# RWKV-5 attention and a routed expert layer on one core: attention output by chunk parity and head, states carried on TensorE and ScalarE

## The chip, the core and the metric

The kernel runs on one core of one Trainium2 chip. The metric is the device time of one execution in microseconds (us). Three executions of the kernel before took 550.02, 550.48 and 550.54 us, so its time is the median, 550.48 us. The profile is of one more execution, which took 550.23 us.

The engines are called as in the profile: PE is TensorE, PEld its weight loads, DVE is VectorE, ACT is ScalarE, POOL is GpSimd, SP issues transfers. An f32 matmul of the program leaves two records in the profile (it runs as two passes), a PE transpose leaves one.

## What is computed

The first part is RWKV-5 attention with 4 batches, 8 heads, 768 tokens and a head width of 48:

```python
for t in range(S):
    kt, vt, rt = (k[:, :, t], v[:, :, t], r[:, :, t])
    cur = np.einsum('bhd,bhe->bhde', u[None] * kt, vt)
    y[:, :, t] = np.einsum('bhd,bhde->bhe', rt, state + cur)
    state = w[None, :, :, None] * state + np.einsum('bhd,bhe->bhde', kt, vt)
```

The second part takes y as x (4 x 768 tokens, 384 wide). It forms nine logits for each token (eight experts and one local gate), picks an expert by the largest logit or keeps the token before's expert where the gate says so, sends each token through its expert (384 to 1024, relu, 1024 to 384) and scales the result by the softmax probability.

## The kernel before

There are three stages: attention (`chunked_attention`), routing (`route`) and the experts (`experts`). Only the attention stage is changed, with the layout of its inputs. All work is in f32.

Attention runs over 16 **items**, each one batch and one pair of heads. The two heads of a pair lie on partitions 0 to 47 and 64 to 111; each head is padded from 48 to 64 (`DP`). The 768 tokens are cut into six chunks of 128. Powers of the decay w are made once at the start (`pw`, its reciprocal `inv`, and `endT`, which weights a key by what is left of it at the end of its chunk).

For one item `first` does this:

- POOL scales r by `pw` into `rw` (L112), k by `endT` into `ke` (L114), and multiplies r and k into `pd` (L115). DVE scales k by `inv` into `kw` (L113).
- PE forms what each of five chunks adds to the state, for both heads at once, into `ds` (L120). DVE then walks the recurrence: for each chunk and head it multiplies the state by w to the 128th and adds `ds` (L128 for the first chunk, L130 for the four others), into `st`. The state tile is block-diagonal, 128 x 128 with zeros between the heads.
- PE forms the scores inside each chunk, one head on each half of the array's rows (`sc`, L141), and DVE masks them into `am` (L144).
- PE sums `pd` weighted by u (`dp`, L152), and DVE multiplies that by v transposed into `own` (L154): the token's own term.

`second` follows one item later. PE applies the states to `rw` (`yp`, L163) and the masked scores to v, one head on each half of the array's columns (`yp`, L169). DVE adds `own` and writes `xT` (L172). After the four items of a batch `finish` turns `xT` by 24 PE transposes (`tp`, L180), ACT copies them into `x` (L181), which goes to memory, eight matmuls form the nine logits (`lp`, L189), ACT copies them (`lT`, L191), six small transposes turn them (`lq`, L194), and DVE writes `lt` (L196).

Each item's five inputs (rT, kT, k, v, vT, all padded to 64 per head, 384 KB each) are loaded by SP into one of three buffers. Eight PSUM banks are shared by all the matmul outputs of the stage. A scheduler decides the final order of the instructions on each engine from the order in which the program writes them.

## Time and profile before

| what | number |
|---|---|
| median of three executions | 550.48 us |
| the profiled execution | 550.23 us |
| its span, first to last instruction | 548.5 us |
| busy share of the span: PE, DVE, POOL, ACT | 89%, 36%, 29%, 10% |
| first `ds` matmul of the first item | 19.19 us |
| `lt` of the last batch written (end of attention) | 182.20 + 0.21 us |
| mean granted TensorE clock | 0.952 |

The span has 1.7 us around it. Attention takes the first 182 us, routing with the first gathers lasts until 221.8 us, and the experts fill the rest with PE busy throughout. The clock is granted in full through the attention stage, at half during most of routing.

A timeline row gives the start, the time from the start of a run of like instructions to the end of its last one, the engine, the line, and how many records it merges. Matmuls are pipelined, so such rows overlap: what a group costs on PE is the distance from its start to the start of the next group.

### The profile page before, as it was taken

The numbers are of one execution on the slowest core, as the hardware profiler recorded it, in microseconds if no ns is written. First come the engines' busy times: TensorE is split into PE (matmuls) and PEld (weight loads), VectorE is DVE, ScalarE is ACT, GpSimd is POOL, SyncE is SP. The second block draws the span as 40 slices with busy tenths as digits, with TensorE's granted clock in tenths as the row PEclk, the third lists the DMA queues.
The fourth block names the chain that finished last, engine by engine and source line by source line (L and its number), as shares of the span: only waits on it lengthen the run. The fifth ranks groups of instructions, "written<-read, shape, count | busy, mean of one in ns | idle before, by whom it ended". The sixth has DMA issues, their size and how long they took to land.

```text
span 548.5 us, 6145 instructions
## 1 busy us (share of the span) xinstructions
PE 487.6 (89%) x2358; PEld 291.7 (53%) x2358; DVE 197.4 (36%) x467; ACT 55.7 (10%) x106; POOL 161.1 (29%) x138
## 2 busy tenths in 40 slices
PE   0689999999999435999999999999999999999990
PEld 0577677577577134455555555555555555555540
DVE  6799859769765561001111111112011111111010
ACT  0000200200201000011111101111101111011110
POOL 6678547357320113302122121221221210201102
PEclk9999999999999755799999999999999999999995
DMA  8678866755410841203514306206117016000001
GB/s 293 244 260 269 270 212 240 241 192 192 141 33 23 346 178 50 79 9 104 197 34 157 137 27 208 92 25 246 56 30 272 28 36 232 29 1 23 14 2 52
DMA packets 21653, 72.34 MB, mean 132 GB/s; under 512 B 3543, under 2 KB 6778, under 8 KB 19568
## 3 DMA queue, kind: packets, MB, share of 16 engines
q1 hardware_dynamic: 13824, 56.63, 29.4%
q0 software_dynamic: 3840, 10.23, 5.7%
q10 hardware_dynamic: 3952, 5.00, 2.5%
q8 instruction: 21, 0.34, 0.3%
q14 instruction: 16, 0.13, 0.1%
HBM read 62.41 MB, written 10.22 MB: 132 GB/s over the span
## 4 chain that ended last, share of the span: by engine, by line
issue 52%; DVE 18%; PE 15%; POOL 12%; DMA 1%; POOLq 1%; ACT 0%
POOL out_dram L544 6%; DVE st L130 5%; POOL xg L500 5%; PE lp L189 4%; DVE kw L113 4%; DVE am L144 4%; PE mp L461 2%; PE tp L180 2%; PE yp L169 2%; DVE xT L172 2%; DVE own L154 2%; PE yp L163 2%; PE ds L120 1%; PE sc L141 1%; DVE st L128 1%
## 5 line engine op out<-in xcount | busy, mean ns | idle before, releaser
L518 PE MATMUL h<-exT,w1t 128*128 128x448 f32 x384 | 155.6, 545 | 0.0
L528 PE MATMUL y<-hT,w2t 128*128 128x448 f32 x384 | 155.4, 541 | 0.0
L518 PEld LDWEIGHTS h<-exT,w1t 128*128 128x128 f32 x384 | 72.2, 193 | 64.7 <-issue 64.7
L528 PEld LDWEIGHTS y<-hT,w2t 128*128 128x128 f32 x384 | 70.2, 190 | 58.8 <-issue 58.3
L544 POOL DMA_INDIRECT out_dram<-yo,sid x32 | 31.3, 978 | 174.6 <-DVE yo L542 174.0
L513 DVE COPY exT<-etp 128x384 f32<-128x384 f32 (+1 forms) x32 | 16.2, 508 | 132.6 <-PE etp L512 131.7
L521 ACT ACTIVATE hT<-h 128x448 f32<-128x448 f32 x64 | 34.8, 544 | 285.4 <-PE h L518 242.9
L542 DVE TENSOR_SCALAR yo<-otp,gate 128x384 f32<-128x384 f32 (+1 forms) x32 | 19.5, 615 | 118.7 <-PE otp L540 118.6
L500 POOL DMA_INDIRECT xg<-x_d,gid x32 | 32.4, 1013 | 101.4 <-PE etp L512 85.4
L112 POOL TENSOR_TENSOR rw<-rT,pw 128x768 f32<-128x768 f32 x16 | 28.8, 1798 | 43.2 <-PE yp L163 42.3
L130 DVE SCALAR_TENSOR_TENSOR st<-st,pw,ds 64x64 f32<-64x64 f32 x128 | 35.9, 280 | 4.1
L115 POOL TENSOR_TENSOR pd<-rT,kT 128x768 f32<-128x768 f32 x16 | 29.8, 1860 | 16.5 <-PE dp L152 12.5
L114 POOL TENSOR_TENSOR ke<-k,endT 128x768 f32<-128x768 f32 x16 | 32.5, 2031 | 6.7 <-POOL rw L112 3.1
L144 DVE TENSOR_TENSOR am<-sc,mask 128x384 f32<-128x384 f32 x64 | 31.2, 551 | 0.5
L141 PE MATMUL sc<-rw,kw 64*128 64x128 f32 x384 | 27.1, 290 | 2.3 <-POOL rw L112 2.3
L169 PE MATMUL yp<-am,v 128*64 128x128 f32 x384 | 28.9, 281 | 0.0
L120 PE MATMUL ds<-v,ke 128*128 128x128 f32 x160 | 23.1, 294 | 6.0 <-POOL ke L114 6.0
L163 PE MATMUL yp<-rw,st 128*128 128x128 f32 x160 | 25.5, 290 | 1.4 <-DVE st L130 1.4
L141 PEld LDWEIGHTS sc<-rw,kw 64*128 64x128 f32 x384 | 23.9, 196 | 4.4 <-POOL rw L112 2.6
L163 PEld LDWEIGHTS yp<-rw,st 128*128 128x128 f32 x160 | 20.8, 190 | 9.0 <-PE dp L152 4.2
L181 ACT COPY x<-tp 128x384 f32<-128x384 f32 x24 | 11.2, 480 | 141.8 <-PE tp L180 141.6
L152 PE MATMUL dp<-pd,uz 128*128 128x384 f32 x64 | 25.0, 513 | 0.0
(132 smaller groups left out, 308.6 us busy)
## 6 DMA issues: line engine op xcount, KB each, us to landing
w1t<-in_w_dram SPq DMA_DIRECT2D x8, 1536.0 KB, 6.6
w2t<-in_w_dram SPq DMA_DIRECT2D x8, 1536.0 KB, 8.4
rT<-in_rT_dram SPq DMA_DIRECT2D x16, 384.0 KB, 4.8
kT<-in_kT_dram SPq DMA_DIRECT2D x16, 384.0 KB, 5.8
k<-in_k_dram SPq DMA_DIRECT2D x16, 384.0 KB, 6.2
v<-in_v_dram SPq DMA_DIRECT2D x16, 384.0 KB, 4.1
vT<-in_vT_dram SPq DMA_DIRECT2D x16, 384.0 KB, 3.3
x_d<-x ACTq DMA_DIRECT2D x4, 1152.0 KB, 6.0
```

What stands on the lines that cost most here:

```text
L114: nc.gpsimd.tensor_mul(ke, t["k"], spread(endT[:, hp], 1, NCH))
L115: nc.gpsimd.tensor_mul(pd, t["rT"], t["kT"])
L130: nc.vector.scalar_tensor_tensor(state[q, c, i], state[q, c - 1, i], pw[q, hp, P:P + 1], add, Alu.mult, Alu.add)
L141: nc.tensor.matmul(sc[i][:, c * P:(c + 1) * P], lhsT=kw[q, g + c, :], rhs=rw[q, g + c, :], start=True, stop=True)
L144: nc.vector.tensor_mul(am[:, i, g:g + 3], sc[i][:, :3 * P].rearrange("p (c t) -> p c t", t=P), spread(mask, 1, 3))
L163: nc.tensor.matmul(yp[:, c % 3 * P:(c % 3 + 1) * P], lhsT=t["state"][:, c - 1].rearrange("p i e -> p (i e)"), rhs=t["rw"][:, c, :], start= ...
L169: nc.tensor.matmul(yp[i * DP:(i + 1) * DP, c % 3 * P:(c % 3 + 1) * P], lhsT=t["v"][:, c, i * DP:(i + 1) * DP], rhs=t["am"][:, i, c, :], st ...
L500: nc.gpsimd.indirect_dma_start(out=xg[:n], out_offset=None, in_=x_d, in_offset=bass.IndirectOffsetOnAxis(ap=gid[:n, e * ST + j:e * ST + j ...
L518: nc.tensor.matmul(h[:, :CAP], lhsT=t[e]["w1"][:, m, kk, :], rhs=t[e]["xT"][:, kk, :], start=(kk == 0), stop=(kk == DK - 1))
L521: nc.scalar.activation(hT, h[:, :CAP], Act.Relu)
L528: nc.tensor.matmul(t[e]["y"][d][:, :CAP], lhsT=t[e]["w2"][:, m, d * P:(d + 1) * P], rhs=t[e][m], start=(m == 0), stop=(m == FK - 1))
L544: nc.gpsimd.indirect_dma_start(out=outs[c], out_offset=bass.IndirectOffsetOnAxis(ap=sid[:n, c:c + 1], axis=0), in_=yo[:n], in_offset=None, ...
```

## The change

Attention is written anew around quarters of the array.

- **Tokens by chunk parity.** The output y of one head takes one PSUM bank: even chunks on partitions 0 to 63, odd chunks on 64 to 127. So `inside` (scores times v) uses one half of the array's columns for each parity, and `before` (states times `rw`) and `own` (u times `pd`) use quarters: 64 rows (a head) by 64 columns (a parity). `xT` holds 8 heads by 384 columns in place of 4 pairs by 768.
- **States on PE and ACT.** The state has 64 rows by 64 columns for each head, with no zero blocks. `added` forms the five additions into one bank `T` (64 x 64 for each matmul) and ACT copies the first one out to `S`. `chain(n, c)` multiplies `S` of the chunk before by a diagonal of w to the 128th (`wd`) on PE, accumulating onto `T`, and ACT copies the sum to `S`. DVE no longer touches the states.
- **Logits** of a batch are 16 matmuls with 32 columns each, two row halves by four column groups; `gather` adds the parts by multiplying with `sel`.
- **Turning** is done by `turn` for each item (six transposes, two ACT copies) and not for a whole batch.
- **Loads.** r and k come in one tile and transfer (`rk`), k and v by token without padding (`kv`), and v transposed by parity (`vT`), in four buffers. From the fifth item on, `rk` and `vT` are loaded as two transfers of 48 partitions each, which leaves the padding rows of the first loads in place. `ke` has 576 columns in place of 768.
- The program order of an iteration n is set in the loop at the end: `turn(n-2)`, `added(n)`, `inside(n-1)`, `chain 1`, `before(n-1)`, `chain 2`, `own(n)`, `chain 3`, half of the scores, `chain 4`, the other half; then `logits` or `gather` in the iterations that follow a batch.
- The input layout, made on the host, and the fallback for unusual decays read the new tensors; the fallback does not run on these inputs.

```diff
-        ps = pool("ps", 8, space=PSUM)
+        three = pool("three", 3)
+        ps = pool("ps", 7, space=PSUM)
+        pst = pool("pst", 1, space=PSUM)
...
+        def load(n):
+            b, hp = divmod(n, HP)
+            rk, vT, kv = rks[n % NB], vTs[n % NB], kvs[n % NB]
+            for t, src in ((rk, rk_d), (vT, vT_d)):
+                flat = t.rearrange("p a c t -> p (a c t)")
+                if n < NB:
+                    nc.sync.dma_start(out=flat, in_=src[b, hp])
+                else:
+                    for i in range(2):
+                        q = slice(i * DP, i * DP + DH)
+                        nc.sync.dma_start(out=flat[q], in_=src[b, hp, q])
+                if t is rk:
+                    nc.sync.dma_start(out=kv, in_=kv_d[b, hp])
...
-        sts = [once.tile([P, NCH - 1, 2, DP], F32, name=f"st{i}") for i in range(2)]
-        for z in sts:
-            for i in range(2):
-                nc.gpsimd.memset(z[i * DP:(i + 1) * DP, :, 1 - i, :], 0.0)
...
+        endT = once.tile([P, HP, 2, DH], F32, name="endT")
...
+        halves = once.tile([P, DP], F32, name="halves")
+        nc.vector.tensor_add(halves, ident[:, :DP], ident[:, DP:])
+        wd = once.tile([P, HP, DP], F32, name="wd")
+        nc.vector.tensor_mul(wd, spread(halves, 1, HP), pw[:, :, P:P + 1].to_broadcast([P, HP, DP]))
+        sel = once.tile([P, E + 1], F32, name="sel")
+        nc.vector.tensor_reduce(sel, ident.rearrange("p (j i) -> p i j", j=4)[:, :E + 1], axis=AX.X, op=Alu.add)
...
+        def scale(n):
+            t = items[n]
+            t["ke"] = two.tile([P, NCH, 2 * DH], F32, name="ke")
+            t["pd"] = two.tile([P, NCH, P], F32, name="pd")
+            t["rw"] = three.tile([P, NCH, P], F32, name="rw")
+            hp = t["hp"]
+            nc.gpsimd.tensor_mul(t["ke"], t["k"], spread(endT[:, hp].rearrange("p i d -> p (i d)"), 1, NCH))
+            nc.gpsimd.tensor_mul(t["pd"], t["rT"], t["kT"])
+            nc.gpsimd.tensor_mul(t["rw"], t["rT"], spread(pw[:, hp, :P], 1, NCH))
+        def added(n):
+            t = items[n]
+            t["kw"] = two.tile([P, NCH, P], F32, name="kw")
+            nc.vector.tensor_mul(t["kw"], t["kT"], spread(inv[:, t["hp"]], 1, NCH))
+            t["T"] = pst.tile([P, NCH - 1, DP], F32, name="T")
+            t["S"] = three.tile([P, NCH - 1, DP], F32, name="S")
             for c in range(NCH - 1):
+                for h in range(2):
+                    nc.tensor.matmul(t["T"][h * DP:(h + 1) * DP, c], lhsT=t["ke"][:].rearrange("p c x -> p (c x)")
+                                     [:, (2 * c + h) * DH:(2 * c + h) * DH + DP],
+                                     rhs=t["v"][:, (2 * c + h) * DH:(2 * c + h) * DH + DP],
+                                     start=(c == 0), stop=(c == 0), skip_group_check=True)
+            nc.scalar.copy(t["S"][:, 0], t["T"][:, 0])
...
+        def chain(n, c):
+            t = items[n]
+            for h in range(2):
+                q = slice(h * DP, h * DP + DH)
+                nc.tensor.matmul(t["T"][h * DP:(h + 1) * DP, c], lhsT=wd[q, t["hp"]], rhs=t["S"][q, c - 1],
+                                 start=False, stop=True, skip_group_check=True)
+            nc.scalar.copy(t["S"][:, c], t["T"][:, c])
...
+        def own(n):
+            for p in range(2):
+                for h in range(2):
+                    q = slice(h * DP, h * DP + DH)
+                    nc.tensor.matmul(dp[h][p * DP:(p + 1) * DP, :C2 * P].rearrange("p (c t) -> p c t", c=C2),
+                                     lhsT=w_t[q, t["hp"], 1:2].to_broadcast([DH, DP]),
+                                     rhs=t["pd"][q].rearrange("p (c k) t -> p k c t", k=2)[:, p],
+                                     start=True, stop=True)
...
+        def scores(n, g):
+            sc = [bank("sc") for _ in range(2)]
+            for c in range(3):
+                for h in range(2):
+                    q = slice(h * DP, h * DP + DH)
+                    nc.tensor.matmul(sc[h][:, c * P:(c + 1) * P], lhsT=t["kw"][q, 3 * g + c],
+                                     rhs=t["rw"][q, 3 * g + c], start=True, stop=True)
...
+        def inside(n):
+            t = items[n]
+            t["y"] = [bank("yp") for _ in range(2)]
+            for h in range(2):
+                for c in range(NCH):
+                    p, c2 = c % 2, c // 2
+                    nc.tensor.matmul(t["y"][h][p * DP:(p + 1) * DP, c2 * P:(c2 + 1) * P],
+                                     lhsT=t["v"][:, (2 * c + h) * DH:(2 * c + h) * DH + DP], rhs=t["am"][:, h, c],
+                                     start=(c2 == 0), stop=False, skip_group_check=True)
...
+        def before(n, xT):
+            t = items[n]
+            for c in range(1, NCH):
+                p, c2 = c % 2, c // 2
+                for h in range(2):
+                    q = slice(h * DP, h * DP + DH)
+                    nc.tensor.matmul(t["y"][h][p * DP:(p + 1) * DP, c2 * P:(c2 + 1) * P],
+                                     lhsT=t["S"][q, c - 1], rhs=t["rw"][q, c],
+                                     start=False, stop=True, skip_group_check=True)
+            for h in range(2):
+                nc.vector.tensor_add(xT[:, 2 * t["hp"] + h], t["y"][h][:, :C2 * P],
+                                     t["own"][:, h].rearrange("p c t -> p (c t)"))
...
+        def turn(n, xT, x):
+            for h in range(2 * items[n]["hp"], 2 * items[n]["hp"] + 2):
                 tp = bank("tp")
-                for hp in range(HP):
-                    nc.tensor.transpose(tp[:, hp * P:(hp + 1) * P], xT[:, hp, c * P:(c + 1) * P], ident)
-                nc.scalar.copy(x[:, c].rearrange("p (h e) -> p h e", h=H),
-                               tp.rearrange("p (h e) -> p h e", h=H)[:, :, :DH])
+                for c2 in range(C2):
+                    nc.tensor.transpose(tp[:, c2 * P:(c2 + 1) * P], xT[:, h, c2 * P:(c2 + 1) * P], ident)
+                nc.scalar.copy(x[:, :, h * DH:(h + 1) * DH],
+                               tp[:, :C2 * P].rearrange("p (c e) -> p c e", e=DP)[..., :DH])
...
-            lT = two.tile([E + 1, S], F32, name="lT")
-            for g in range(2):
-                z = slice(g * S // 2, (g + 1) * S // 2)
-                lp = bank("lp")
-                for hp in range(HP):
-                    nc.tensor.matmul(lp[:E + 1, :S // 2], lhsT=wp[:, hp, :], rhs=xT[:, hp, z],
-                                     start=(hp == 0), stop=(hp == HP - 1))
+            lT = two.tile([P, 2, C2 * P], F32, name="lT")
+            lp = [bank("lp") for _ in range(2)]
+            for h in range(H):
+                for p in range(2):
+                    q, j = slice(p * DP, (p + 1) * DP), h % 4
+                    nc.tensor.matmul(lp[p][32 * j:32 * j + 32, :C2 * P], lhsT=wp[q, h], rhs=xT[q, h],
+                                     start=(h < 4), stop=(h >= 4))
+            for p in range(2):
+                nc.scalar.copy(lT[:, p], lp[p][:, :C2 * P])
...
+        def gather(b, lT):
             lq = bank("lq")
             for c in range(NCH):
-                nc.tensor.transpose(lq[:, c * (E + 1):(c + 1) * (E + 1)], lT[:, c * P:(c + 1) * P],
-                                    ident[:E + 1, :E + 1])
-            nc.vector.tensor_copy(lt[:, b * NCH:(b + 1) * NCH, :].rearrange("p c e -> p (c e)"),
-                                  lq[:, :NCH * (E + 1)])
+                nc.tensor.matmul(lq[:, c * (E + 1):(c + 1) * (E + 1)], lhsT=lT[:, c % 2, c // 2 * P:(c // 2 + 1) * P],
+                                 rhs=sel, start=True, stop=True)
+            nc.scalar.copy(lt[:, b * NCH:(b + 1) * NCH, :].rearrange("p c e -> p (c e)"), lq[:, :NCH * (E + 1)])
...
+        scale(0)
+        for n in range(M + 2):
+            if n + 2 < M:
+                load(n + 2)
+            if n - 2 >= 0:
+                b = items[n - 2]["b"]
+                turn(n - 2, xTs[b], xs[b])
+            if n < M:
+                added(n)
+                if n % HP == 0:
+                    xTs[n // HP] = two.tile([P, H, C2 * P], F32, name="xT")
+                    xs[n // HP] = two.tile([P, NCH, D], F32, name="x")
+            if n + 1 < M:
+                scale(n + 1)
+            if 0 <= n - 1 < M:
+                inside(n - 1)
+            if n < M:
+                chain(n, 1)
+            if 0 <= n - 1 < M:
+                before(n - 1, xTs[items[n - 1]["b"]])
+            if n < M:
+                chain(n, 2)
+                own(n)
+                chain(n, 3)
+                scores(n, 0)
+                chain(n, 4)
+                scores(n, 1)
+            if n >= 2 and (n - 2) % HP == HP - 1:
+                b = items[n - 2]["b"]
+                lTs[b] = logits(b, xTs[b], xs[b])
+                if n == M + 1:
+                    gather(b, lTs[b])
+            elif n - 3 >= 0 and (n - 3) % HP == HP - 1:
+                gather(items[n - 3]["b"], lTs[items[n - 3]["b"]])
```

In the order of PE's instructions, an item between two batch ends stood like this before (`st_108` and `st_109` are the two state tiles):

```order
L120 MATMUL ds<-v,ke 128x128 x5
L141 MATMUL sc<-rw,kw 128x128 x12
L152 MATMUL dp<-pd,uz 128x384 x2
L163 MATMUL yp<-rw,st_108 128x128 x2
L169 MATMUL yp<-am,v 64x128 x6
L163 MATMUL yp<-rw,st_108 128x128 x3
L169 MATMUL yp<-am,v 64x128 x6
```

and stands like this now (`T` from `kv` and `ke` is `added`, `T` from `S` and `wd` is a `chain` step, `yp` from `kv` is `inside`, `yp` from `S` is `before`, `dp` is `own`):

```order
L222 MATMUL tp<-ident,xT 128x128 x6
L148 MATMUL T<-kv_117,ke 64x64 x10
L200 MATMUL yp<-am,kv_116 64x128 x12
L159 MATMUL T<-S,wd 64x64 x2
L210 MATMUL yp<-rw,S 64x128 x10
L159 MATMUL T<-S,wd 64x64 x2
L171 MATMUL dp<-pd,w_t 64x384 x4
L159 MATMUL T<-S,wd 64x64 x2
L188 MATMUL sc<-rw,kw 128x128 x6
L159 MATMUL T<-S,wd 64x64 x2
L188 MATMUL sc<-rw,kw 128x128 x6
```

The transposes of the item two back come first; the four chain steps stand apart, each with other matmuls of PE behind it; the output shape (the first number is the rows written) changes six times in an item, as often as before.

In the iteration that also forms a batch's logits, PE's order is this now, behind the transposes, `added` and `inside`:

```order
L210 MATMUL yp<-rw,S 64x128 x10
L171 MATMUL dp<-pd,w_t 64x384 x2
L159 MATMUL T<-S,wd 64x64 x2
L171 MATMUL dp<-pd,w_t 64x384 x2
L188 MATMUL sc<-rw,kw 128x128 x2
L159 MATMUL T<-S,wd 64x64 x2
L188 MATMUL sc<-rw,kw 128x128 x2
L159 MATMUL T<-S,wd 64x64 x2
L188 MATMUL sc<-rw,kw 128x128 x2
L159 MATMUL T<-S,wd 64x64 x2
L188 MATMUL sc<-rw,kw 128x128 x6
L233 MATMUL lp<-xT,wp 32x384 x16
```

Here the scheduler has put the chain later: three of its steps stand inside the scores, two score matmuls apart.

At the start of the stage DVE's order before was

```order
L89 RECIPROCAL inv<-pw 128x512
L91 TENSOR_TENSOR end<-inv,pw 128x512
L113 TENSOR_TENSOR kw<-kT,inv 128x768 x2
L96 COPY endT<-ep 128x512
L128 COPY st_108<-ds 64x64 x2
```

and it is now (`halves`, `wd` and `sel` are the new constants)

```order
L112 RECIPROCAL inv<-pw 128x512
L122 TENSOR_TENSOR halves<-ident 128x64
L114 TENSOR_TENSOR end<-inv,pw 128x512
L124 TENSOR_TENSOR wd<-halves,pw 128x256
L126 TENSOR_REDUCE sel<-ident 128x9
L143 TENSOR_TENSOR kw<-rk_107,inv 128x768
L119 COPY endT<-ep 128x384
L143 TENSOR_TENSOR kw<-rk_108,inv 128x768
```

`endT`, for which the first `ke` on POOL waits, has moved ahead of the second `kw`.

178 lines of the change are left out of this document (54 added, 124 removed).

## The prediction

> **What bounds the kernel now.** I began with the table of busy time by stretch, because the change touches only the first 182 us.
>
> ```profile
> core 0: us, PE busy (x) PEld busy (x) DVE busy (x) ACT busy (x) POOL busy (x), PEclk, DMA share, GB/s
> 40.00:60.00 20.00, 19.46 (x206) 15.89 (x202) 19.36 (x45) 0.00 (x0) 16.56 (x9) 1.00 0.82 277
> 60.00:80.00 20.00, 19.28 (x145) 12.28 (x142) 11.93 (x35) 3.77 (x8) 7.39 (x5) 1.00 0.73 240
> ```
>
> Two kinds of stretch alternate. Between batch ends PE and DVE are both nearly full (19.46 and 19.36 of 20 us); at a batch end PE stays full while DVE falls to 11.93 us and POOL to 7.39. So DVE can at most be the second bound, and a batch end costs PE time that nothing else shares. The timeline prices each group. The last two items and the end of attention, with the start behind them:
>
> ```profile
> 155.53 1.38 PE L120 MATMUL ds<-v,ke 128*128 128x128 f32 x10
> ...
> 162.78 1.38 PE L120 MATMUL ds<-v,ke 128*128 128x128 f32 x10
> 163.76 0.48 DVE L128 COPY st<-ds 64x64 f32<-64x64 f32 x2 [0.30 <-PE ds L120]
> 164.10 1.61 PE L141 MATMUL sc<-rw,kw 64*128 64x128 f32 x24
> 164.26 2.47 DVE L130 SCALAR_TENSOR_TENSOR st<-st,pw,ds 64x64 f32<-64x64 f32 x8
> 165.63 1.56 PE L152 MATMUL dp<-pd,uz 128*128 128x384 f32 x4
> 166.76 1.95 DVE L144 TENSOR_TENSOR am<-sc,mask 128x384 f32<-128x384 f32 x4
> 167.03 0.61 PE L163 MATMUL yp<-rw,st 128*128 128x128 f32 x4
> 167.57 0.88 PE L169 MATMUL yp<-am,v 128*64 128x128 f32 x12
> 168.37 0.94 PE L163 MATMUL yp<-rw,st 128*128 128x128 f32 x6
> 168.63 1.01 DVE L154 TENSOR_TENSOR own<-dp,vT 128x384 f32<-128x384 f32 x2
> 169.24 0.88 PE L169 MATMUL yp<-am,v 128*64 128x128 f32 x12
> 169.56 1.16 DVE L172 TENSOR_TENSOR xT<-yp,own 128x384 f32<-128x384 f32 x2
> ...
> 173.16 2.84 PE L180 MATMUL tp<-ident,xT 128*128 128x128 f32 x24
> 175.93 5.33 PE L189 MATMUL lp<-xT,wp 128*9 128x384 f32 x16
> 181.19 0.35 PE L194 MATMUL lq<-ident,lT 9*128 9x9 f32 x3
> 181.30 0.47 ACT L191 COPY lT<-lp 9x384 f32<-9x384 f32 x1 [2.11 <-PE lp L189]
> 181.82 0.35 PE L194 MATMUL lq<-ident,lT 9*128 9x9 f32 x3 [0.28 <-ACT lT L191]
> 182.20 0.21 DVE L196 COPY lt<-lq 128x54 f32<-128x54 f32 x1 [8.37 <-PE lq L194]
> ```
>
> ```profile
> 11.88 4.77 DVE L113 TENSOR_TENSOR kw<-kT,inv 128x768 f32<-128x768 f32 x2
> 16.58 0.68 DVE L96 COPY endT<-ep 128x512 f32<-128x512 f32 x1
> 17.33 3.57 POOL L114 TENSOR_TENSOR ke<-k,endT 128x768 f32<-128x768 f32 x2 [1.49 <-DVE endT L96]
> 19.19 2.50 PE L120 MATMUL ds<-v,ke 128*128 128x128 f32 x10 [6.00 <-POOL ke L114]
> ...
> 25.97 1.28 PE L120 MATMUL ds<-v,ke 128*128 128x128 f32 x10
> ```
>
> Read starts, not lengths. A plain item takes 162.78 - 155.53 = 7.25 us, with PE's groups close behind each other. From the second item's `ds` (25.97) to the last one's (162.78) are 136.8 us for 14 items, 9.77 each: the batch ends hold the difference. Such an end is 24 transposes (173.16 to 175.93, 2.77 us), 16 logit passes (to 181.19, 5.26 us), and about 1.2 us to `lt`. Attention ends at 182.41, 19.6 us after the last `ds`.
>
> **Prices.** A full-array pass of 128 columns costs 2.77 / 24 = 0.115 us, one of 384 columns 5.26 / 16 = 0.33. The 24 score passes, on the two row halves by turns, take 164.10 to 165.63 = 1.53 us; one at a time they would be 2.76, two at once 1.38. So halves run at the same time, and about 0.15 us is left for the change of shape. The column halves agree (12 passes, 167.57 to 168.37, 0.80 us: 0.69 + 0.11), and so does `ds` (10 passes, 1.32: 1.15 + 0.17). I take 0.15 for each change of shape. A pass of 64 columns isn't in the trace: half of 0.115 is 0.06, and three `lq` records of 9 columns take 0.35, so at most 0.12; I take 0.08, nearer to the wide pass by size.
>
> **The new item on PE**, in its order, from these prices:
>
> - `turn`: 6 transposes, 0.69 + 0.15 = 0.84 (moved out of the batch end, not added).
> - `added`: 20 short passes in column pairs, 10 x 0.08 + 0.15 = 0.95 (0.75 to 1.35).
> - `inside`: 24 passes in pairs, same shape, 12 x 0.115 = 1.38.
> - Four `chain` steps of two passes in time, 0.16 each; the first and the last change the shape: 0.94.
> - `before`: 20 passes over four quarters, at most six on one: 0.69. In pairs it would be 1.15.
> - `own`: 8 passes of 384 columns, four at once: 0.66. In pairs 1.32.
> - Scores: two halves of 0.69 + 0.15: 1.68.
>
> That is 7.14 us. No row has four quarters at once; the bounds are four and two at a time, and I take four, since row halves and column halves each already run together at full rate. The Trainium skill says the same for 32 x 32 tiles (TensorE: Matmul & The Clock Gate, Part 3, measured speedup): a pack takes one matmul's time and about 4 ns for each further tile. By it `before` and `own` are 1.35 us together, by pairs 2.47; no run here shows quarters yet.
>
> **The chain's waits** are new on PE's queue, and everything of PE stands behind each. A step's result must drain, be copied by ACT, and come back. The last logits show the way: `lp` ends at 181.26, ACT starts 0.04 later, copies 384 columns in 0.47, and `lq` starts 0.05 after. With about 0.3 us of drain (the 1.38 of `ds` less nine passes) and a copy of 64 columns between 0.21 (the `lt` copy) and 0.47, one step takes 0.6 to 0.86 us. Behind step 1 stands `before` (0.69), behind 2 `own` (0.66), behind 3 half the scores (0.84). The stall is 0 to 0.4 us an item; I take 0.1, since ACT's copy has a sixth of the 384 columns. A plain item is then 7.25 us, what it is now.
>
> **The batch end.** Logits are 32 passes of 384 columns in eight tiles: 4 x 0.33 + 0.15 = 1.47 us (four at a time: 2.8). In that iteration three chain steps stand apart inside the scores, so four more changes of shape: 0.60. `gather` is 12 short passes, 0.96 + 0.15 = 1.11. Together 3.2 us, where now an end costs 2.77 + 5.26 + 1.2 = 9.2 and more.
>
> **The sum.** From the second item to the last: 14 x 7.25 + 3 x 3.2 = 111.1 us in place of 136.8, a gain of 25.7.
>
> At the start, `endT` waits for one `kw` (2.4 us of the 4.77), not two, and for three small constants (0.8, an estimate: three instructions with fewer columns together than `endT`, which takes 0.68); `ke`, with 576 columns for 768, is shorter by a quarter. The first state matmul then starts 1.8 us before 19.19. POOL then makes `pd`, `rw` and `ke` for the second item, ready at about 22.5 us by the rows quoted below, before PE comes to it near 24. I count 1.5 us.
>
> At the end, from the last `added`: 6.4 for the rest of its iteration, 0.84 for a `turn`, 0.4 until the masks are done, 1.53 + 0.84 for the last `inside` and `before`, 0.3 drain, 1.16 for `xT`, 0.84 for the last `turn`, 1.47 logits, 1.24 for two copies, 1.0 `gather`, 0.55 to `lt`: 16.6 in place of 19.6, a gain of 3.0.
>
> Gain 25.7 + 1.5 + 3.0 = 30.2 us. The profiled execution took 550.23 us (548.5 of span and 1.7 around it), 0.25 below the median, so 520 us. Routing and experts, 366 us behind 182.41, are as before.
>
> **What is costed at nothing.** DVE loses 0.48 + 2.47 us an item and keeps 5.6: 1.95, 1.01 and 1.16 above, and `kw`. POOL keeps 5.2. Their rows:
>
> ```profile
> L113 DVE TENSOR_TENSOR kw<-kT,inv 128x768 f32<-128x768 f32 x16 | 23.7, 1484 | 0.0
> L112 POOL TENSOR_TENSOR rw<-rT,pw 128x768 f32<-128x768 f32 x16 | 28.8, 1798 | 43.2 <-PE yp L163 42.3 <-POOL st L75 0.9
> L115 POOL TENSOR_TENSOR pd<-rT,kT 128x768 f32<-128x768 f32 x16 | 29.8, 1860 | 16.5 <-PE dp L152 12.5 <-POOL ke L114 2.5 <-issue 1.5
> L114 POOL TENSOR_TENSOR ke<-k,endT 128x768 f32<-128x768 f32 x16 | 32.5, 2031 | 6.7 <-POOL rw L112 3.1 <-PE ds L120 2.1 <-DVE endT L96 1.5
> rT<-in_rT_dram SPq DMA_DIRECT2D x16, 384.0 KB, 4.8
> ```
>
> Both hide under 7.25 us of PE; if PE were much quicker, DVE at 5.6 would be the next bound, so no more than 1.6 us an item is to be had. Loads fall from 5 x 384 = 1920 KB an item to 576 + 584 + 288 = 1448 (`rk`, `kv`, `vT`) from the fifth on, 1736 before: 5.4 us at 277 GB/s, under the 7.25. Should transfers of 48 partitions run at half that rate, `rk` and `vT` take 6.4 and an item's loads 8.6 us, 1.3 too many for 12 items: 536 us. ACT has seven copies an item, 3.3 us even if each took 0.47.
>
> **Rivals.**
>
> 1. Only two tiles run at a time, also in quarters. For it: the trace shows pairs and nothing more. Against: neither kind of half slows the other's rate. `before` and `own` lose 1.12 us an item (18 us), the logits 5.3 for 1.3 at four ends (16 us): 554 us, slower. It decides where the loss passes 30 us, near 1.9 us an item.
> 2. The two halves of a `chain` step go one after the other. They write the same bank `T`, where the score halves, which run together, write two. Each step then takes 0.16 us more: 4 x 16 x 0.16 = 10 us, 530. The Trainium skill has this as a rule (TensorEngine Tiling (Array Packing), Gotcha 1: PSUM Pressure): different row tiles cannot access the same bank at the same time. No run here shows two row tiles in one bank so far.
> 3. ACT answers late: a round trip of 1.0 us shows 0.3, 0.3 and 0.2 behind the three covers, 0.8 us an item: 12 us, 532. For it: ACT has the copies of `turn` ahead of the first state copy. Against: `inside` (1.38) stands ahead of step 1.
> 4. Faster still: short passes at 0.06 (0.20 less in `added`, 0.16 in the chain) and no stall give 6.8 us an item, and 0.3 less at each batch end: 8.5 us, 511. Nothing speaks against it but that no row has a pass so short.
>
> **How the numbers follow.** The forecast (514 to 527) has 0.50, rival 2 0.13, rival 3 0.14, late loads 0.04, rival 4 0.11, rival 1 0.08. The range 507 to 540 leaves out rival 1, the low end of 4 and mixtures of 2, 3 and late loads. A measurement here tells apart about 0.2%, 1.1 us. Slower by more needs rival 1 or several others together: 0.07; within it 0.03; faster 0.90.
>
> **What would show it.** Right: start-to-start near 7.25 us between `added` of plain items, `own` near 0.7 us with starts of four records nearly together, the batch end near 3 us, `lt` near 152 us, and experts unchanged. Wrong: `own` at 1.3 (rival 1); `chain` records of the two heads 0.16 us apart (rival 2); PE idle behind ACT's `S` above 0.3 us an item (rival 3); PE or POOL waiting for `rk` or `kv` (loads).

## The result, and the profile after

The changed kernel takes **515.42 us** (median of four executions, 514.65 to 515.97), the kernel before, on the same chip, 550.25 us (549.35 to 550.54). The ratio is 0.9369, with a 95% interval of 0.9352 to 0.9385: 34.8 us faster. The prediction was 520 us, with 507 to 540 as its range. The profiled execution has a span of 512.6 us in place of 548.5; it is the fastest of the four (514.65 us), with a mean granted clock of 0.948 where the other three show 0.942.

First the same table of busy time by stretch (columns as before):

```profile
core 0: us, PE busy (x) PEld busy (x) DVE busy (x) ACT busy (x) POOL busy (x), PEclk, DMA share, GB/s
40.00:60.00 20.00, 20.00 (x351) 16.48 (x349) 14.89 (x27) 5.36 (x21) 16.69 (x10) 1.00 0.98 248
80.00:100.00 20.00, 20.00 (x326) 15.81 (x318) 15.44 (x27) 5.16 (x20) 14.92 (x9) 1.00 0.89 225
100.00:120.00 20.00, 19.18 (x336) 15.61 (x334) 14.34 (x23) 5.15 (x20) 12.14 (x9) 1.00 1.00 247
```

PE is now full almost without a gap, DVE has fallen from 19.36 to about 15 of 20 us, and there are no longer stretches of two kinds. The last two columns changed too: the transfer engines are busy 0.89 to 1.00 of the time and move 225 to 248 GB/s, where before they moved 277 and 240 at a share of 0.82 and 0.73.

The timeline of PE: the logits of one batch, its `gather`, and one plain item. What a group costs is the distance to the next group's start.

```profile
60.05 1.52 PE L233 MATMUL lp<-xT,wp 64*32 64x384 f32 x32
61.50 0.87 PE L222 MATMUL tp<-ident,xT 128*128 128x128 f32 x6
...
68.14 1.51 PE L242 MATMUL lq<-sel,lT 128*128 128x9 f32 x12
69.50 0.85 PE L222 MATMUL tp<-ident,xT 128*128 128x128 f32 x6
...
76.12 0.87 PE L222 MATMUL tp<-ident,xT 128*128 128x128 f32 x6
76.92 0.80 PE L148 MATMUL T<-kv,ke 128*64 128x64 f32 x20
77.56 1.48 PE L200 MATMUL yp<-am,kv 128*64 128x128 f32 x24
78.97 0.27 PE L159 MATMUL T<-S,wd 48*64 48x64 f32 x2
...
79.13 0.71 PE L210 MATMUL yp<-rw,S 48*64 48x128 f32 x17
...
79.91 0.81 PE L171 MATMUL dp<-pd,w_t 48*64 48x384 f32 x5
80.42 0.41 PE L159 MATMUL T<-S,wd 48*64 48x64 f32 x4
80.76 0.94 PE L188 MATMUL sc<-rw,kw 48*128 48x128 f32 x12
81.63 0.33 PE L159 MATMUL T<-S,wd 48*64 48x64 f32 x4
81.89 0.94 PE L188 MATMUL sc<-rw,kw 48*128 48x128 f32 x12
82.76 0.88 PE L222 MATMUL tp<-ident,xT 128*128 128x128 f32 x6
83.57 0.63 PE L148 MATMUL T<-kv,ke 128*64 128x64 f32 x14
```

An item takes 82.76 - 76.12 = 6.64 us. The logits take 1.45 us (60.05 to 61.50) and the gather 1.36 (68.14 to 69.50). The logits are one run of 32 passes, where before half as many passes took 5.26 us.

Single records, listed from the trace, show how many tiles run together. Starts in us of the passes of one logits group, of `before`, of the last four passes of `own`, and of the chain steps at 80.42 and 81.63:

```
lp      60.048 60.054 60.061 60.068 60.074 60.081 60.088 60.094 | 60.394 60.401 ...
before  79.134 79.141 79.143 79.163 | 79.246 79.252 79.253 79.272 | ...
own     80.005 80.016 80.103 80.238
T       80.425 80.481 80.560 80.616
T       81.633 81.639 81.739 81.746
```

Eight 64 x 32 tiles start within 0.05 us, and the next eight 0.35 us after the first. In `before` four passes, one for each quarter, start within 0.03 us, and the next four 0.11 us later. The records do not name the half of the array. In the step at 81.63 the starts come in pairs 6 to 7 ns apart, which I read as the two heads together; in the step at 80.42 they come one by one.

The start and the end of attention, where `T` stands for the old `ds`:

```profile
3.70 0.38 SPq L85 DMA_DIRECT2D rk<-in_rk_dram  x1
...
13.83 0.56 DVE L119 COPY endT<-ep 128x384 f32<-128x384 f32 x1
...
16.56 1.33 PE L148 MATMUL T<-kv,ke 128*64 128x64 f32 x20 [1.29 <-POOL ke L135]
...
26.34 1.28 PE L148 MATMUL T<-kv,ke 128*64 128x64 f32 x20
```

```profile
131.41 0.80 PE L148 MATMUL T<-kv,ke 128*64 128x64 f32 x20
...
142.51 0.38 ACTq L227 DMA_DIRECT2D x_d<-x  x1
...
145.82 0.20 ACT L244 COPY lt<-lq 128x54 f32<-128x54 f32 x1 [1.37 <-PE lq L242]
...
147.25 0.35 DVE L394 TENSOR_REDUCE mx<-lt 128x24 f32<-128x192 f32 x1 [5.80 <-DMA x_d<-x]
```

Where the 35.9 us of the span came from, stage by stage (starts of the state matmul of the first, second and last item, end of `lt`, first expert matmul, end of the span):

| stage | before | after | gain |
|---|---|---|---|
| start to the second item | 25.97 | 26.34 | -0.4 |
| second item to the last | 136.8 | 105.1 | 31.7 |
| last item to the end of `lt` | 19.6 | 14.6 | 5.0 |
| `lt` to the first expert matmul (221.79; 186.42) | 39.4 | 40.4 | -1.0 |
| from there to the end | 326.7 | 326.2 | 0.5 |

The profile above shows two things that the forecast didn't have. The first item takes 26.34 - 16.56 = 9.78 us, and its `T` 1.33 us for the work that takes 0.80 later. And the first operation of routing (`mx`) starts 1.23 us behind the end of `lt`, waiting for the write of x, which was issued at 142.51; before, it followed 0.25 us behind `lt`.

### The profile page after: what moved, and what is told of

Same layout as the page of the kernel before. It is cut to its first block, busy times and chain, and to the rows that moved or that the text cites. A ratio compares the mean times of both kernels' runs of the same rounds, so it can differ in the third digit from the quotient of the medians.

```text
span 512.6 us, 7471 instructions
## 1 busy us (share of the span) xinstructions
PE 458.8 (90%) x3086; PEld 279.8 (55%) x3086; DVE 159.5 (31%) x306; ACT 73.2 (14%) x198; POOL 150.4 (29%) x134
## 4 chain that ended last, share of the span: by engine, by line
issue 54%; PE 26%; POOL 12%; DVE 3%; DMA 2%; POOLq 1%; ACT 0%
PE sc L188 6%; POOL out_dram L610 6%; POOL xg L566 5%; PE yp L200 5%; PE T L159 3%; PE tp L222 2%; PE T L148 2%; PE dp L171 2%; PE mp L527 2%; PE yp L210 2%; DMA x_d<-x 1%; PE lp L233 1%; PE lq L242 1%; DVE inv L112 1%; DMA xg<-x_d,gid 1%
## 5 line engine op out<-in xcount | busy, mean ns | idle before, releaser
L587 ACT ACTIVATE hT<-h 128x448 f32<-128x448 f32 x64 | 34.8, 543 | 285.0 <-PE h L584 285.0
L136 POOL TENSOR_TENSOR pd<-rk 128x768 f32<-128x768 f32 x16 | 29.0, 1813 | 20.0 <-issue 7.5
L188 PE MATMUL sc<-rw,kw 48*128 48x128 f32 x384 | 33.4, 303 | 0.0
L137 POOL TENSOR_TENSOR rw<-rk,pw 128x768 f32<-128x768 f32 x16 | 26.9, 1682 | 17.1 <-PE yp L210 17.1
L188 PEld LDWEIGHTS sc<-rw,kw 48*128 48x128 f32 x384 | 25.7, 195 | 4.5 <-issue 1.2
L135 POOL TENSOR_TENSOR ke<-kv,endT 128x576 f32<-128x576 f32 x16 | 26.8, 1676 | 2.5 <-DVE endT L119 2.5
L200 PE MATMUL yp<-am,kv 128*64 128x128 f32 x384 | 26.2, 283 | 0.8 <-issue 0.8
L214 DVE TENSOR_TENSOR xT<-yp,own 128x384 f32<-128x384 f32 x32 | 16.4, 553 | 31.7 <-PE yp L210 31.7
L159 PE MATMUL T<-S,wd 48*64 48x64 f32 x256 | 25.1, 242 | 0.0
L143 DVE TENSOR_TENSOR kw<-rk,inv 128x768 f32<-128x768 f32 x16 | 25.0, 1563 | 0.0
L578 PE MATMUL etp<-ident,xg 128*128 128x128 f32 (+1 forms) x96 | 16.7, 285 | 7.2 <-DMA xg<-x_d,gid 7.1
L200 PEld LDWEIGHTS yp<-am,kv 128*64 128x64 f32 x384 | 22.0, 142 | 1.5 <-issue 1.1
```

The source lines that it names most:

```text
L136: nc.gpsimd.tensor_mul(t["pd"], t["rT"], t["kT"])
L137: nc.gpsimd.tensor_mul(t["rw"], t["rT"], spread(pw[:, hp, :P], 1, NCH))
L159: nc.tensor.matmul(t["T"][h * DP:(h + 1) * DP, c], lhsT=wd[q, t["hp"]], rhs=t["S"][q, c - 1], start=False, stop=True, skip_group_check=True)
L188: nc.tensor.matmul(sc[h][:, c * P:(c + 1) * P], lhsT=t["kw"][q, 3 * g + c], rhs=t["rw"][q, 3 * g + c], start=True, stop=True)
L200: nc.tensor.matmul(t["y"][h][p * DP:(p + 1) * DP, c2 * P:(c2 + 1) * P], lhsT=t["v"][:, (2 * c + h) * DH:(2 * c + h) * DH + DP], rhs=t["am" ...
L578: nc.tensor.transpose(tp[:, kk, :n], t[e]["xg"][j][:n, kk * P:(kk + 1) * P], ident[:n, :n])
```

## The experiments

Ratios are to the kernel before, times medians. The ratio is estimated from executions measured side by side and need not be the quotient of two medians. A run and the change were not measured side by side: the kernel before took 550.09 to 550.82 us beside the runs and 550.25 beside the change. All start from the changed kernel, but for the third, which starts from the kernel before.

### Two tiles at once for the logits

```diff
-   lp[p][32*j:32*j+32, :C2*P], lhsT=wp[q, h], start=(h < 4), stop=(h >= 4)
+   lp[p][:32, :C2*P],          lhsT=wp[q, h], start=(h == 0), stop=(h == H-1)
```

The column groups go, the two row halves stay; `gather` reads 32 rows.

> The changed kernel with the logits of all heads in one column group, so that two tiles work at a time (one for each row half) in place of eight; the last step then reads 32 rows. Theory (eight tiles run at once and a batch end is paid on PE alone): 32 passes take 16 x 0.33 = 5.3 us in place of 1.45, 3.9 us more at four batch ends, 15 us: 531 us. Rival (a batch end's PE time hides behind other engines, or the eight tiles did not really run together): within 3 us of 515.

Measured 531.68 us, 0.9643 (0.9588 to 0.9698). The logits on PE's timeline of this kernel:

```profile
60.38 5.35 PE L233 MATMUL lp<-xT,wp 64*32 64x384 f32 x32
...
66.47 0.80 PE L148 MATMUL T<-kv,ke 128*64 128x64 f32 x20
```

The same 32 records take 5.35 us in place of 1.52, and an iteration with logits 12.61 us in place of 8.78: 3.83 at each of four batch ends, 15.3 of the 16.3 us. So tiles beyond two run together at nearly the full rate (1.45 us for four rounds of 0.33), and without it nearly half of the change is lost.

### The chain of waits away: states on DVE again, but compact

```diff
-   for h in range(2):
-       nc.tensor.matmul(T[h half, c], lhsT=wd[q, hp], rhs=S[q, c - 1], start=False, ...)
-   nc.scalar.copy(S[:, c], T[:, c])
+   nc.vector.scalar_tensor_tensor(S[:, c], S[:, c - 1], pw[:, hp, P:P + 1], T[:, c], mult, add)
```

> The changed kernel with the state recurrence back on DVE: the compact state of both heads in one operation of 128 x 64 for a chunk, no chain matmuls, no state copies on ACT but the first. Theory (PE sets the item at 6.64 us, and the chain costs PE 0.4 us inside the 64 x 64 block and 0.46 us between the halves of the scores): PE falls to 5.8 us, DVE rises by four operations near 0.28 us to some 6.4, the item is about 6.4 and the split chain at a batch end (0.7 us) goes: 510 us. Rival (the gain came from taking the states off DVE): DVE becomes the bound with stalls, the item is 7.2 us or more: 523 us.

Measured 507.9 us, 0.9206 (0.9157 to 0.9256): 7.5 us faster than the change. A plain item falls from 6.64 to 5.84 us, so the four steps cost PE 0.80 an item:

```profile
36.13 0.80 PE L148 MATMUL T<-kv,ke 128*64 128x64 f32 x20
...
41.96 0.80 PE L148 MATMUL T<-kv,ke 128*64 128x64 f32 x20
```

The price on DVE, and who waits now (groups of instructions, then a stretch, then the waits from 25 to 140 us; a wait's row gives its total, how often, and the longest):

```profile
L157 DVE SCALAR_TENSOR_TENSOR S<-S,pw,T 128x64 f32<-128x64 f32 x64 | 17.6, 276 | 5.4 <-ACT S L152 4.3
```

```profile
80.00:100.00 20.00, 17.35 (x280) 13.50 (x280) 15.90 (x35) 3.55 (x11) 12.96 (x8) 0.97 0.88 216
```

```profile
POOL pd L136 <- DMA rk<-in_rk_dram: 14.2, 6, 5.0
...
DVE kw L143 <- DMA rk<-in_rk_dram: 4.7, 3, 3.1
```

Without zero blocks one DVE operation serves both heads of a chunk: 4 x 0.276 = 1.1 us an item, where the old layout took 0.48 + 2.47. The compact layout alone would have taken 1.8 of these 2.95 us from DVE; the move to PE took the other 1.1 and charged PE 0.80. But the gain is 7.5 us and not 16 x 0.80 = 12.8: PE is only 17.35 of 20 us busy in this stretch, and POOL and DVE wait for `rk`. The loads, which kept just ahead of an item of 6.64 us, do not keep ahead of 5.84.

### Only the logits in column groups, on the kernel before

```diff
-   nc.tensor.matmul(lp[:E+1, :S//2], lhsT=wp[:, hp, :], rhs=xT[:, hp, z], start=(hp == 0), stop=(hp == HP-1))
+   nc.tensor.matmul(lp[32*hp:32*hp+32, :S//2], lhsT=wp[:, hp, :], rhs=xT[:, hp, z], start=True, stop=True)
```

`wp` is padded to 32 columns, and the six small transposes become matmuls with `sel`.

> The kernel before with one part of the change alone: the logits of the four pairs in four column groups, four tiles at once, and the parts added by the matrix of ones as in the changed kernel. Theory (a batch end is PE time that nothing covers): 16 passes of 0.33 us become 4, 5.26 to 1.5 us, the gather is 0.7 us dearer: 3.1 us at four ends, 12 us: 538 us. Rival (DVE or the loads bound the batch end too): less than 4 us, above 546.

Measured 540.07 us, 0.9826 (0.9796 to 0.9855): 10.0 us less than the kernel before took beside it (550.09), and 2 less than the 12 or so expected. The end of attention of this kernel shows what is missing:

```profile
165.78 0.38 ACTq L185 DMA_DIRECT2D x_d<-x  x1
...
168.27 0.21 DVE L198 COPY lt<-lq 128x54 f32<-128x54 f32 x1 [5.21 <-PE lq L196]
170.80 0.35 DVE L330 TENSOR_REDUCE mx<-lt 128x24 f32<-128x192 f32 x1 [2.32 <-DMA x_d<-x]
```

In this profile attention ends 13.9 us earlier than in the kernel before (168.48 for 182.41), and 2.3 us of that turn into a wait for the write of x, the same wait as in the change: the long logits had hidden it. So of the 34.8 us about 10 come from the logits alone; the rest needs the other parts.

### The first load not behind the check of the decay

```diff
-   ok = fl.tile([P, 2, HP], F32, name="ok")      # likewise some, one
+   ok = keep.tile([P, 2, HP], F32, name="ok")
```

In the change the loads' tiles take the space of the check's, so the first load is issued at 3.70 us (0.81 in the kernel before).

> The changed kernel with the three small tiles of the decay check put where nothing reuses their space, so that the first load needn't wait for the check (it went out at 3.70 us, before the change at 0.81). Theory (the first state matmul waits for endT, and that for the decay powers, which wait for the small transfer of w; without the loads beside it that transfer landed at 2.8 us in place of 4.5): the first product on POOL starts 2.5 us earlier, but the chain to endT starts later; first state matmul between 15.5 and 17.5 us, total 514 to 516.5. Rival (the late loads cost the head 2.9 us): first state matmul near 14 us, total near 512.5.

Measured 516.54 us, 0.9381 (0.9353 to 0.941): no gain. The first load is issued at 0.81 us, but the first `T` comes at 17.30 and the second at 27.09, later by 0.7 in this one profile. DVE, which waits for the small transfer of w, starts its first operation on it at 5.25 us where the change does so at 2.79, and `endT` follows at 14.57 in place of 13.83. So `endT` and `ke` set the first item, not the loads.

### Whole loads in place of two of 48 partitions

```diff
-   if n < NB:
+   if True:
```

> The changed kernel with all loads of r, k and transposed v over 128 partitions, padding included, also from the fifth item on: 1736 KB an item in place of 1448. Theory (loads hide under 6.64 us of PE): no change that can be told, 514.5 to 516. Rival (the transfer engines, busy 0.88 to 1.00 through the plain items, are the next bound): 288 KB more at 248 GB/s are 1.2 us an item for 12 items, some 14 us, 529; and if transfers of 48 partitions are the poorer ones, less busy engines and no change or a small gain.

Measured 515.76 us, 0.9369 (0.9348 to 0.939): no change that the time could tell. In this profile the clock was granted at 0.86 and 0.79 in the two stretches from 65 to 75 us, with PE busy throughout, which made two items some 1.6 us longer; the change's profile has 1.00 there, so a gain of that size could be hidden. But the transfers themselves differ. Two stretches of this kernel, then its issues (count, KB each, median us to landing), then those of the change:

```profile
80.00:100.00 20.00, 20.00 (x346) 15.80 (x344) 13.24 (x26) 5.16 (x20) 13.71 (x9) 1.00 0.92 312
100.00:120.00 20.00, 20.00 (x346) 16.62 (x345) 12.65 (x24) 5.35 (x21) 13.49 (x10) 1.00 0.45 156
```

```profile
rk<-in_rk_dram SPq DMA_DIRECT2D x16, 768.0 KB, 7.1
kv<-in_kv_dram SPq DMA_DIRECT2D x16, 584.0 KB, 5.0
```

```profile
kv<-in_kv_dram SPq DMA_DIRECT2D x16, 584.0 KB, 7.8
rk<-in_rk_dram SPq DMA_DIRECT2D x24, 288.0 KB, 7.3
```

With whole loads `kv` lands in 5.0 us and `rk`, 768 KB at once, in 7.1; in the change each 288 KB half of `rk` takes 7.3 and `kv` 7.8. The engines move 312 GB/s at a busy share of 0.92, and have half of the last stretch to spare (0.45), though they move 20% more bytes (1736 KB an item for 1448). A single row of `rk` (one partition, 6144 bytes) takes 480 ns in the change and 234 here, the medians of the trace's packet records from 80 to 100 us. Leaving out the padding made the loads slower, and PE, the bound, hid it. The edit takes away two things at once, the 48 partitions and the second transfer; which of them counts is not separated.

### Both: states on DVE and whole loads

The two edits above together.

> The changed kernel with the states on DVE (as in the second experiment) and with loads over all 128 partitions. Theory (with the states on DVE the loads became the bound: POOL and DVE waited 14.2 and 4.7 us for r and k there, the transfer engines were busy 0.88 to 0.95 at 216 to 236 GB/s; transfers over 128 partitions move more bytes in less time, 312 GB/s): the long items (6.7 to 9.3 us where 5.84 is the plain one) go, second to last item 98.1 to about 91 us, 501 us. Rival (more bytes take more time): 288 KB more an item, 515 us; or the long items come from elsewhere: 508.

Measured 502.53 us, 0.912 (0.9094 to 0.9146). From the second item to the last it takes 93.0 us where 91 were expected (98.1 with the states on DVE and the loads as in the change, 105.1 in the change itself; about 1.5 of the 98.1 are an item at a lower clock, 0.86 and 0.80 in the stretches from 95 to 105 us). The waits for `rk` are gone; one for `kv` is left (from 25 to 128 us):

```profile
POOL ke L135 <- DMA kv<-in_kv_dram: 12.3, 4, 4.0
```

Three items still take 6.33, 6.91 and 6.96 us where a plain one takes 5.84. The 12.9 us gained on the change lie beside the 12.8 that 16 x 0.80 makes, but that is partly luck: iterations with logits lose the split chain as well (7.29 to 7.60 for 8.78), the first item is shorter (8.19 for 9.78), and the long items take some of it back.

### The fourth chain step behind the scores

```diff
-   chain(n, 4)
-   scores(n, 1)
+   scores(n, 1)
+   chain(n, 4)
```

> The changed kernel with the fourth chain step behind all scores and not between their halves. Theory (PE bound, and each change of shape costs PE): two changes of shape fewer between the score halves, one more behind them, 0.2 to 0.3 us an item, 3 to 5 us in all: 511 us. Rival (the next item's additions then wait for the last state copy, since there is one bank T): no gain, 515, or slower.

Measured 513.32 us, 0.9329 (0.9303 to 0.9354). This interval overlaps that of the change, and the profiled execution, 514.89 us, is no faster than the change's; the trace settles the price of the plain item. There PE does:

```profile
80.14 0.41 PE L159 MATMUL T<-S,wd 48*64 48x64 f32 x4
80.48 1.61 PE L188 MATMUL sc<-rw,kw 48*128 48x128 f32 x24
82.02 0.33 PE L159 MATMUL T<-S,wd 48*64 48x64 f32 x4
82.28 0.87 PE L222 MATMUL tp<-ident,xT 128*128 128x128 f32 x6
```

The scores are one run of 1.54 us in place of 0.87 + 0.87, and the item takes 6.44 us: one change of shape fewer, 0.20 us. I had priced it at 0.15. Only some 2 of the 4 us expected arrived in the time. Part of the rest is the clock, at least in this profile: it was granted at 0.85 and 0.81 in the two stretches from 125 to 135 us, and the last `T` there takes 1.33 us for 0.80.

### The tiles of x not reused by routing

```diff
-   xs[n // HP] = two.tile([P, NCH, D], F32, name="x")
+   xs[n // HP] = xk[n // HP % 2]      # two tiles that live on through routing
```

> The changed kernel with the two x tiles in space that the routing stage doesn't reuse. Theory (routing starts 1.2 us after the last logits are written, since its first tiles take space that the write of x still reads): the start comes 1.0 us earlier, 514.4 us. Rival (another wait stands behind it, or the loads of the weights): no change, 515.4.

Measured 514.99 us, 0.936 (0.9337 to 0.9382), not to be told from the change by the time alone. In the profile the wait is gone:

```profile
145.48 0.20 ACT L244 COPY lt<-lq 128x54 f32<-128x54 f32 x1 [1.37 <-PE lq L242]
145.71 0.35 DVE L394 TENSOR_REDUCE mx<-lt 128x24 f32<-128x192 f32 x1
```

So routing had waited because its tiles lie where x was being read by the write. Together with the two edits above it was run once more:

> The one before with the x tiles in space of their own as well. Theory (routing then starts right behind the last logits): 1.1 us less than the one before, 500 us. Rival (the wait returns elsewhere): the same as the one before.

Measured **500.35 us**, 0.909 (0.9062 to 0.9118): the fastest version here, 15 us below the change. Its intervals with and without the kept tiles overlap (502.53 and 500.35).

### PE kept busy from the start

```diff
+   for _ in range(32):
+       nc.tensor.matmul(warm[:, :P], lhsT=ident, rhs=ident, start=True, stop=True)
    load(0)
```

The product is not used. It asks whether the slow first item is the clock's.

> The changed kernel with 32 matmuls of the identity that nothing reads, on PE between the decay check and the first transposes, while PE has nothing else to do. Theory (the first item takes 9.78 us, not for its order but since PE runs at half speed there: 20 passes of its additions take 1.33 us, later 0.80): it falls to 6.5 to 7 us and the total by about 3, 512.5 us. Rival (the chain of the first item, drawn out over the scores, sets its length): 9 us or more and no change, 515.4.

Measured 518.11 us, 0.9419 (0.9384 to 0.9454): slower, a miss. Granted clock and the first item of this kernel:

```profile
15.00:20.00 5.00, 0.14 (x2) 0.15 (x4) 3.79 (x4) 0.00 (x0) 3.64 (x3) 0.83 1.02 413
20.00:25.00 5.00, 5.00 (x42) 3.36 (x42) 1.22 (x3) 0.21 (x1) 4.86 (x4) 0.50 1.05 340
```

```profile
17.78 0.55 DVE L122 COPY endT<-ep 128x384 f32<-128x384 f32 x1
...
19.86 1.33 PE L151 MATMUL T<-kv,ke 128*64 128x64 f32 x20 [5.31 <-POOL ke L138]
...
29.63 1.28 PE L151 MATMUL T<-kv,ke 128*64 128x64 f32 x20
```

The edit did two things more than it was meant to: the scheduler put both halves of the second `kw` ahead of the copy of `endT` (17.78 in place of 13.83 us), so `T` came 3.3 us later, and PE, idle for 5.3 us before it, fell back to half of its clock. It answers the question all the same. At a granted clock of 0.50 the first item takes 29.63 - 19.86 = 9.77 us, what it takes in the change (9.78), and its `T` the same 1.33. The slow first item is an item at half the clock. On the fastest version the same edit fared as badly:

> States on DVE, loads over 128 partitions, x tiles in space of their own and the 32 matmuls at the start, all together. Theory: the gains add, 3 us below the kernel without the 32 matmuls, near 497 us. Rival (an earlier start only meets loads that have not landed): as without them, 500 us.

Measured 503.58 us, 0.9134 (0.91 to 0.9167), 3 us above the version without it: `T` at 19.84 in place of 16.89 us.

## Why the prediction was right, and where it was wrong

**The time** came out 4.6 us below the forecast and inside the range, and inside the forecast's own 514 to 527. The mechanism, quarters at full rate, held; its terms erred to both sides, by 8 us to the better (middle and end) and by 3 to the worse (start and routing). That the sum came so near is in part luck.

**The plain item**, 7.25 forecast, measured 6.64. Part by part (forecast, measured): `turn` 0.84, 0.80; `added` 0.95, 0.64; `inside` 1.38, 1.41; the first three chain steps, `before` and `own` together 1.98, 1.79; score halves 0.84, 0.87 each; the last step 0.31, 0.26; stall 0.1, none on PE (in front of step 3 the weight loads wait 0.32 us for ACT's copy, until 80.37, while passes of `own` still run). What was mis-sized is the **short pass**. I chose 0.08 us between 0.06 and 0.12; ten pairs in 0.64 - 0.15 make 0.05. In the step at 80.42 passes that follow one another stand 0.056 us apart, half of the 0.11 between rounds of 128 columns: half the columns cost half the time. That was rival 4's premise, and it was true; its price of 511 was missed because of the losses below. The wide `own` and `before` came as priced: with short passes at 0.056 the forecast of 1.98 becomes 1.84, and 1.79 were measured. For `before` the four quarters show in the starts. `own` takes 0.79 us from its first record (79.633) to the next step, and its starts are not the four together that the prediction named as a sign; two at a time would have been 1.32.

The changes of shape were counted by rows read and rows written together (48*64, say): six in an item before and six now. By rows written alone, as the text above the prediction puts it, it would be four and four.

**The batch end**, 3.2 forecast. The iterations with logits and with gather take 8.78 and 7.98 us, 2.14 and 1.34 above a plain one: 3.5. Logits 1.45 for 1.47, the split chain 0.69 for 0.60, the gather 1.34 for 1.11.

**From the second item to the last**: 14 x 0.61 = 8.5 us less than forecast, 3 x 0.3 = 0.9 more, and 1.65 more in two single items of 7.25 and 7.68 us (the first ends the stretch of half clock, in the second PE sits 0.8 us before its `inside` behind nothing that the profile names). That gives the 105.1 measured for 111.1 forecast.

**The start** was wrong in sign: 1.5 us of gain forecast, 0.4 of loss measured. The first `T` did come earlier, 16.56 for 19.19, more than the 1.8 forecast. The step that failed is "before PE comes to it near 24": I priced the first item at the full clock, and wrote that it is granted in full through the attention stage. A row that I had quoted spoke against it: the first `ds` takes 2.50 us and the next 1.28. PE's clock, not POOL, was the limit, and the change put more PE work into the first item, because `own`, the scores and the chain all stand there, so the half clock cost it more.

**The end**: 3.0 forecast, 5.0 measured (14.6 us for 16.6). The rest of the last item takes 5.8 for 6.4; the masks are done when PE comes to them (0.4); `inside`, `before` and the drain take 0.3 less, `xT` and the last `turn` overlap (0.4), and the copies and the gather behind the logits take 2.5 for 2.8.

**Routing** was forecast as unchanged and lost 1.0. What the sum left out is the write of x: it is issued behind the last `turn`, as before, but the logits that used to hide it are 3.8 us shorter. A transfer lost its cover. Two other runs agree, one that removes the wait, and one that makes the logits short in the kernel before and pays 2.3 us.

**The rivals.** (1), only two tiles at a time, fell by the records that start together and by the logits at two tiles, which cost 3.83 us a batch end. (2), the heads of a chain step one after the other in one bank, fell as a rule: in 37 of the 64 steps the starts come in pairs 6 to 7 ns apart, and the step at 81.63 takes 0.26 us with its change of shape, where 0.31 was priced for both together and 0.47 apart (0.26 and 0.37 with short passes at 0.056). The Trainium skill (TensorEngine Tiling (Array Packing), Gotcha 1: PSUM Pressure) says that different row tiles cannot access one bank at the same time; for row tiles that write different partitions of it, this trace disagrees in these 37 steps. In the other 27 steps, all of them beside `own`, the second head starts 0.13 to 0.43 us behind the first, and step 3 takes 0.34 us up to the scores. The bank is the same in both kinds of step. At 80.425 and 80.560 the heads start 0.322 us behind each of the last two passes of `own` (80.103 and 80.238), which is the length of a pass of 384 columns. So I read it as a wait for parts of the array that `own` still holds; no run separates that from other causes. (3), ACT late, is bounded by one row of the waits from 26 to 147 us:

```profile
PEld T L159 <- ACT S L161: 3.9, 12, 0.3
```

That is 3.9 us in 12 waits, one of 0.32 in each of 12 items, in front of step 3, where `own` still runs; 12 us would have been needed. The late loads (0.04) didn't stall PE in the change: no row of these waits names a transfer of `rk`, `kv` or `vT`. But they were nearer than I thought: an item 0.8 us shorter met them at once, in the run with the states on DVE.

**Costed at nothing.** The relief of DVE was rightly worth nothing by itself: giving the states back to DVE made the kernel faster. Whether the states had to leave DVE at all was never weighed. It should have been a rival for the design, since 0.94 us of PE was in my own sum for it.

**Open** stays what decides when the full clock comes. The trace's first record of it stands 5.5 us behind the first state matmul in the kernel before (24.7 us), 12.7 behind it in the change (29.2), 6.7 in the version with the states on DVE and whole loads, and 12.9 in the fastest, which differs from that one only in where x lies. In the five other versions of the change with the states on PE and no matmuls at the start it is 10.9 to 12.8, in the other one with the states on DVE 6.8. One profile each does not settle it. (Ahead of that first record the tables by stretch show 1.00 in the change; only the durations say that it was less.) A version that keeps PE busy without delaying `endT` was not run.

## What to carry to other kernels

Where an engine with many small matmuls sets the end, count the array's quarters and column groups that each matmul leaves empty: filled with independent tiles they ran at nearly the full rate here, up to eight together, and one batch of logits fell from 5.3 to 1.5 us. Before work is moved to another engine to relieve one, first look at what the new layout leaves of it: the compact states cost DVE 1.1 us an item, and on PE, the bound, 0.8. And whenever a long group at the end of a stage is shortened, look for the transfer that it was hiding.

## What was not expected of the hardware

- Transfers of 48 partitions are slow for what they carry: each 288 KB half of `rk` takes 7.3 us to land, where 768 KB on 128 partitions take 7.1; at nearly the same busy share (0.89 and 0.92) the stretch from 80 to 100 us moves 225 GB/s in the one kernel and 312 in the other. I had feared half the rate; three quarters of it is what these rows show. Whether the 48 partitions or the cut into two transfers does it is open.
- Two matmuls on different row halves ran together into different partitions of one PSUM bank, accumulating, with starts 6 to 7 ns apart in 37 of the 64 chain steps.
- PE can stay at about half of its clock through 12.7 us of steady work: in the change, from the first state matmul until the first record of the full clock, its 20 short passes take 1.33 and 1.28 us where they take 0.80 later.
- The clock can fall to half for 3.4 us in the middle of attention. The clock records of five of the eleven experiments show it, once each and twice in the run with the early first load; in four of them PE was busy throughout. Neither the change's profile nor that of the kernel before has it. Two items around such a stretch are 1.6 us longer in the run with whole loads, so a difference of 2 us between two executions can be the clock alone.
